# Last product of a three-stage kernel: which operand stays in the array, and how its result is stored

## The chip, the cores and the metric

One core of a Trainium2 chip runs the kernel. The metric is the device time of one execution in microseconds (us). Engines are named as the profile names them: PE (TensorE, matmul), PEld (its weight loads), DVE (VectorE), ACT (ScalarE), POOL (GpSimd), and SP (SyncE), which here only issues DMAs.

## The reference

Three stages follow each other. A chunked linear attention gives a matrix x of 3072 tokens by 256 features; two feed-forward blocks follow:

```python
h = x @ w_in                      # 3072x256 @ 256x2048
x2 = (np.maximum(h, 0)**2) @ w_out      # 2048 -> 256
a = x2 @ w1;  b = x2 @ w2         # 256 -> 1024 each
out = (a * b @ w3) @ w_out2       # 1024 -> 1024 -> 256
```

All of it is float32.

## The kernel before

**Tiles and phases.** Tokens are worked in six tiles of 512 (`TT`, `NTILE`). A tile t has a phase A of 16 steps (`h_mm` L825: 128 hidden features of the first block; `x2_mm` L856: their share of x2) and a phase B of 8 steps (`a_mm` L891, `b_mm` L899, their product, and `out_mm` L907: its share of the output). The order is A0, A1, B0, B1, then A2, B2, A3, B3 and so on to B5 (`PHASES`, L945). "Step A8" is the ninth step of a phase A. The two weights w3 and w_out2 are multiplied with each other in the kernel once (`w3_product`, L251), giving `w3o` of 1024 x 256; the last product is then (a * b) @ w3o.

**Precision.** Each operand is held as a high and a low part (`split`, L143: ACT makes the high part, DVE the rest, `split_lo`). One product is three matmuls, `PASSES` (low x high, high x high, high x low). The parts of a step's activations are a tile `gp` (L134), made by `part_hi` (ACT, L846) and `part_lo` (DVE, L141); the pool has four buffers (`GPB`), given out in turn and free again when the last reader is done.

**Order of the work.** `second` (L1162) runs the second product of a step three steps behind the first (`LAG`), so the last three `out_mm` of a tile lie in the first three steps of the next phase A (for tile 0, of B1). After the last of them `out_evac` (L937) empties the two accumulators, and the next tile's `x2_mm` takes those two PSUM banks (`ps_acc`, two buffers). The compiler's scheduler fixes each engine's order at build time from its own estimate of the times; each engine then runs its list in order, waiting on semaphores.

**The last product before.** In `out_mm` 128 tokens of `gp` are stationary and the 256 columns of `w3o` move: four groups of tokens by three passes, 12 matmuls a step. The result has tokens on the partitions, so ACT copies each accumulator to a `tmp` tile and it is stored in rows of 1 KB, two DMAs a tile. The last tile (t = 5) is finished by `out_last` (L926), group by group.

**What lies beside it.** All DMAs go to SP's queue, in program order (`dma`, L92). While the feed-forward blocks run, the attention of the next tile is made piecewise at fixed slots of the phases (`attention_plan`, L963). A unit of B and C is split into a `gp` buffer and stored to DRAM (`unit_split`, L490, tensor `hl_d`), read back in two arrangements (`unit_bc`, L533, tiles `bt` and `cb`), the decays `e` are loaded (`unit_e`, L514), masked on POOL (L556) and multiplied on DVE (L621). In phases A2, A3 and A4 the first unit of the next tile is split in step A2 (slot 4), the step of `out_evac`; the second unit's split takes a `gp` buffer at slot 13.

Of the kernel before, what the change touches and what calls it, by code (L numbers as in the profile page):

```python
# [7 lines left out]
F32 = mybir.dt.float32  # L8
# [7 lines left out]
P = 128  # L16
# [5 lines left out]
NT, DM, DFF, DF2 = NB * S, H * D, 2048, 1024  # L22
TT = 512
UT = 256
NTILE = NT // TT
KM = DM // P
# [6 lines left out]
MF2 = DF2 // P  # L33
NSUB = TT // P
# [24 lines left out]
def kernel(  # L59
# [19 lines left out]
    nc = tc.nc  # L79
# [12 lines left out]
    def dma(out, in_):  # L92
        tc.keep_in_program_order(nc.sync.dma_start(out=out, in_=in_))  # L93
# [37 lines left out]
    def new_tmp():  # L131
        return tmp.tile([P, 512], F32, tag="tmp", name="tmp")

    def new_gp():  # L134
        return gp.tile([P, 2, 512], F32R, tag="gp", name="gp")

    def new_mm():
        return ps_mm.tile([P, 512], F32, tag="mm", name="mm")

    def split_lo(hi, lo, src):  # L140
        return nc.vector.tensor_tensor(out=lo, in0=src, in1=hi.bitcast(F32), op=ALU.subtract)  # L141

    def split(hi, lo, src):  # L143
        nc.scalar.copy(hi, src)
        split_lo(hi, lo, src)
# [8 lines left out]
    wa, w12, w3, w3o = {}, {}, {}, {}  # L154
# [59 lines left out]
    def conv_parts(i):  # L214
        kind, j = PIECES[i]
        v = cv.pop(i)
        if kind == "o":
            if j == 0:
                wo2.append(act1.tile([P, N_O, 512], F32R, tag="xt", name="wo2"))
            if j % 2 == 0:  # L220
                wo2l[0] = at.tile([P, 2, 512], F32R, tag="e", name="wo2l")
            w = wo2[0][:, j], wo2l[0][:, j % 2]
            split(*w, v)
            wo2.append(w)
            return
        w = wts.tile([P, 2, 512], F32R, tag=PLACE[j % 8] if kind == "3" else f"w{kind}{j}", name=f"w{kind}{j}")
        if kind == "a" and j > 2:
            nc.gpsimd.tensor_copy(w[:, 0, :], v)
        else:
            nc.scalar.copy(w[:, 0, :], v)  # L230
        split_lo(w[:, 0, :], w[:, 1, :], v)
        KEPT[kind][j] = w
        if kind == "3" and j % 2:
            w3_product(j // 2)
# [16 lines left out]
    def w3_product(f):  # L251
        acc = new_mm()
        n = 0
        for e in range(MF2):
            v = w3[2 * f + e // 4]
            for l, r in PASSES:
                nc.tensor.matmul(  # L257
                    acc[:, :DM], v[:, l, e % 4 * P:(e % 4 + 1) * P],
                    wo2[1 + e // 2][r][:, e % 2 * DM:(e % 2 + 1) * DM],
                    start=(n == 0), stop=(n == 3 * MF2 - 1)  # L260
                )
                n += 1
        if f % 2 == 0:
            w3o[f // 2] = wts.tile([P, 2, 2, DM], F32R, tag=f"wo{f // 2}", name=f"w3o{f // 2}")
        w = w3o[f // 2]
        split(w[:, 0, f % 2, :], w[:, 1, f % 2, :], acc[:, :DM])

# [541 lines left out]
    PASSES = ((1, 0), (0, 0), (0, 1))  # L811
# [42 lines left out]
    acc = {}  # L854
# [25 lines left out]
    prods = {}  # L880
# [26 lines left out]
    def out_mm(t, m, subs=range(NSUB), done=True):  # L907
        if m == 0:
            acc["o"] = [ps_acc.tile([P, 2, DM], F32, tag="acc", name="acc") for _ in range(NSUB // 2)]
            if t == NTILE - 1:  # L910
                acc["o"] += [ps_g.tile([P, 2, DM], F32, tag="g", name="acc") for _ in range(NSUB // 2)]
        g = prods[t, m]
        per = NSUB // len(acc["o"])
        for sub in subs:
            for n, (l, r) in enumerate(PASSES):
                i = nc.tensor.matmul(  # L916
                    acc["o"][sub // per][:, sub % per, :], g[:, l, sub * P:(sub + 1) * P], w3o[m // 2][:, r, m % 2, :],
                    start=(m == 0 and n == 0 and sub % per == 0), stop=(m == MF2 - 1 and n == 2),
                    skip_group_check=True,
                )  # L920
                if not done:
                    keep(i)
        if done:
            del prods[t, m]

    def out_last(t):  # L926

        ms = [k[2] for k in late]
        late.clear()
        for sub in range(NSUB):  # L930
            for m in ms:
                out_mm(t, m, (sub,), False)
            o = new_tmp()[:, :DM]
            nc.scalar.copy(o, acc["o"][sub][:, 0])
            dma(out=out[t * TT + sub * P:t * TT + (sub + 1) * P, :], in_=o)

    def out_evac(t):  # L937
        for j in range(NSUB // 2):
            o = new_tmp().rearrange("p (s e) -> p s e", s=2)
            nc.scalar.copy(o, acc["o"][j])  # L940
            r0 = t * TT + 2 * j * P
            dma(out=out[r0:r0 + 2 * P, :].rearrange("(s p) e -> p s e", p=P), in_=o)


    PHASES = [("A", 0), ("A", 1), ("B", 0), ("B", 1)] + [(ph, t) for t in range(2, NTILE) for ph in "AB"]  # L945
# [216 lines left out]
    def second(n, flush=None):  # L1162

        while late and (len(late) > n or (flush and any(k[:2] == flush for k in late))):
            ph, t, m = late.pop(0)
            if ph == "A":
                if flush and m == MF - 2 and (ph, t) == flush:
                    late.pop(0)
                    for e in range(KM):
                        x2_mm(t, m, (e,), True)  # L1170
                        x2_mm(t, m + 1, (e,), True)
                        x2_evac(t, e)
                    continue
                x2_mm(t, m)
                if m == MF - 1:
                    for e in range(KM):
                        x2_evac(t, e)
            else:
                out_mm(t, m)
                if m == MF2 - 1:  # L1180
                    out_evac(t)
# [42 lines left out]
    for ph, t, m in SEQ:  # L1224
# [3 lines left out]
        else:  # L1228
            step(ph, t, m)
    parts()  # L1230
    out_last(NTILE - 1)


# [62 lines left out]
```

## Time and profile before

| | us |
|---|---|
| median of 3 runs | 561.94 (561.61 to 562.13) |
| the profiled execution | 561.75 |
| its span, first to last instruction | 560.0 |
| PE busy | 546.9 (98%) |
| PEld / DVE / ACT / POOL busy | 460.3 / 361.9 / 288.7 / 88.6 |
| matmuls of `out_mm` in all | 576 |
| DMA, share of 16 engines' span | 35.5% |

The profiled execution is 0.19 us below the median, and 1.75 us of it lie outside its span. A matmul's own length in the profile includes the filling and emptying of the array and overlaps the next one; the rate is read from start to start. TensorE's granted clock is 0.996 of full speed on the mean.

### The profile page before, as it was taken

To read this page: it belongs to the slowest core of one execution; us is meant where nothing else is said; L and a number is where in the kernel's file an instruction comes from. 1 tells how busy PE (TensorE), PEld (TensorE's weight loads), DVE (VectorE), ACT (ScalarE), POOL (GpSimd) and SP (SyncE) were. 2 spreads that over 40 slices of the span, in tenths; PEclk is the share of its full clock that TensorE was granted. 3 is DMA by queue.
4 is the path that set the end of the run, shared out by engine and by line. 5 is a ranking of instruction groups with operands and counts; after the bars stand their busy time and mean duration, and the time that the engine had idled before them with its cause. 6 is when DMAs were issued, how large, how long until landed. Compare 5 with 4: busy or idle time off the path is not lost.

```text
span 560.0 us, 9614 instructions
## 1 busy us (share of the span) xinstructions
PE 546.9 (98%) x3580; PEld 460.3 (82%) x3580; DVE 361.9 (65%) x655; ACT 288.7 (52%) x553; POOL 88.6 (16%) x136
## 2 busy tenths in 40 slices
PE   8979999999999999999999999999999999999997
PEld 6757777888888888888888888888888888888886
DVE  5799998977898555466476456474456574545431
ACT  6799768787884342444343444342535332544332
POOL 8264730000001240013030003020012010000000
PEclk9989999999999999999999999999999999999999
DMA  8797690253446470075250066020162220100001
GB/s 240 248 288 249 213 389 7 74 153 107 156 149 169 102 198 1 15 191 143 58 142 1 29 165 148 22 78 1 52 175 77 57 68 1 39 1 1 1 1 37
DMA packets 48735, 59.49 MB, mean 106 GB/s; under 512 B 22960, under 2 KB 36784, under 8 KB 48688
## 3 DMA queue, kind: packets, MB, share of 16 engines
q1 hardware_dynamic: 48688, 58.88, 35.5%
q8 instruction: 28, 0.46, 0.4%
q14 instruction: 19, 0.16, 0.1%
HBM read 50.20 MB, written 8.65 MB: 105 GB/s over the span
## 4 chain that ended last, share of the span: by engine, by line
PE 81%; DVE 8%; DMA 5%; ACT 3%; SPq 1%; issue 1%; DVEq 0%; ACTq 0%
PE mm L816 43%; PE acc L863 18%; PE acc L916 12%; PE mm L257 4%; PE y L752 2%; DVE gp L141 2%; PE g L615 2%; DMA hl_d<-gp 1%; DMA hl_d<-hl 1%; SPq L93 1%; DVE wa L141 1%; DMA raw<-in_raw_dram 1%; DVE cvs L207 1%; DMA u<-in_w_dram 1%; DVE cvs L210 1%
## 5 line engine op out<-in xcount | busy, mean ns | idle before, releaser
L816 PE MATMUL mm<-xt,wa 128*128 128x512 f32 x576 | 148.6, 396 | 3.2 <-DVE wa L141 2.0
L846 ACT CAST gp<-tmp 128x512 fp32r<-128x512 f32 x144 | 89.4, 621 | 115.3 <-DVE tmp L904 63.6
L863 PE MATMUL acc<-gp,wa 128*128 128x512 f32 x576 | 145.9, 392 | 1.3 <-DVE gp L141 0.7
L141 DVE TENSOR_TENSOR gp<-tmp,gp 128x512 fp32r<-128x512 f32 x144 | 103.6, 720 | 61.1 <-ACT gp L846 60.8
L816 PE MATMUL mm<-x,w 128*128 128x512 f32 x576 | 142.6, 393 | 0.0
L816 PEld LDWEIGHTS mm<-xt,wa 128*128 128x128 f32 x576 | 106.4, 190 | 25.8 <-ACT tmp L830 2.4
L863 PEld LDWEIGHTS acc<-gp,wa 128*128 128x128 f32 x576 | 106.5, 188 | 24.5 <-DVE gp L141 1.5
L816 PEld LDWEIGHTS mm<-x,w 128*128 128x128 f32 x576 | 104.5, 188 | 20.5 <-ACT tmp L896 0.2
L830 ACT ACTIVATE tmp<-mm 128x512 f32<-128x512 f32 x96 | 57.3, 596 | 50.8 <-PE mm L816 50.4
L916 PEld LDWEIGHTS acc<-w3o,gp 128*128 128x128 f32 x576 | 75.8, 190 | 4.6 <-DVE gp L141 0.3
L916 PE MATMUL acc<-w3o,gp 128*128 128x256 f32 x576 | 78.5, 283 | 0.1
L840 DVE TENSOR_TENSOR tmp<-tmp 128x512 f32<-128x512 f32 x68 | 47.5, 699 | 29.8 <-ACT tmp L830 28.5
L904 DVE TENSOR_TENSOR tmp<-tmp,mm 128x512 f32<-128x512 f32 x48 | 32.9, 686 | 48.5 <-PE mm L816 44.9
L556 POOL TENSOR_SCALAR_AFFINE_SELECT e<-e 96x768 f32<-96x768 f32 x26 | 25.8, 1005 | 235.8 <-DMA e<-e_d 228.7
L896 ACT COPY tmp<-mm 128x512 f32<-128x512 f32 x48 | 28.1, 586 | 45.9 <-PE mm L816 45.6
L575 POOL TENSOR_TENSOR xb<-xb,dec 96x256 f32<-96x256 f32 x32 | 23.1, 723 | 94.6 <-DMA xb<-in_xb_dram 93.6
L621 DVE TENSOR_TENSOR e<-g,e 128x384 f32<-128x384 f32 x52 | 27.6, 551 | 6.0 <-PE g L615 4.7
L257 PE MATMUL mm<-wo,w 128*128 128x256 f32 x128 | 23.7, 284 | 0.9 <-DVE w L141 0.9
L257 PEld LDWEIGHTS mm<-wo,w 128*128 128x128 f32 x128 | 20.6, 191 | 2.5 <-DVE w L141 1.5
L742 DVE SCALAR_TENSOR_TENSOR xb<-xb,through,y 32x64 f32<-32x64 f32 x72 | 20.4, 283 | 2.8 <-PE y L714 1.1
L615 PEld LDWEIGHTS g<-cb,bt 96*128 96x128 f32 x96 | 16.1, 190 | 2.8
L257 PE MATMUL mm<-wo2l,w 128*128 128x256 f32 x64 | 18.1, 283 | 0.0
(109 smaller groups left out, 447.2 us busy)
## 6 DMA issues: line engine op xcount, KB each, us to landing
u<-in_w_dram SPq DMA_DIRECT2D x24, 512.0 KB, 4.4
ua<-in_w_dram SPq DMA_DIRECT2D x16, 512.0 KB, 6.8
e<-e_d SPq DMA_DIRECT2D x40, 192.0 KB, 4.6
xb<-in_xb_dram SPq DMA_DIRECT2D x32, 192.0 KB, 3.7
bt<-hl_d SPq DMA_DIRECT2D x78, 48.0 KB, 2.0
hl_d<-gp SPq DMA_DIRECT2D x9, 384.0 KB, 2.5
cb<-hl_d SPq DMA_DIRECT2D x66, 48.0 KB, 2.0
out_dram<-tmp SPq DMA_DIRECT2D x10, 256.0 KB, 2.9
```

What stands on the lines that cost most here:

```text
L141: return nc.vector.tensor_tensor(out=lo, in0=src, in1=hi.bitcast(F32), op=ALU.subtract)
L257: nc.tensor.matmul(acc[:, :DM], v[:, l, e % 4 * P:(e % 4 + 1) * P], wo2[1 + e // 2][r][:, e % 2 * DM:(e % 2 + 1) * DM], start=(n == 0), st ...
L615: nc.tensor.matmul(ps[:, 2 * pp:2 * pp + 2], w, un["c2"][:, pr, :, j * CH:(j + 1) * CH], start=True, stop=True)
L621: nc.vector.tensor_tensor(out=m, in0=ps, in1=m, op=ALU.mult)
L816: i = nc.tensor.matmul(ps, w[m][:, l, col + k * P:col + (k + 1) * P], rhs[k][:, r, :], start=((l, r, k) == (1, 0, 0)), stop=((l, r, k) == ...
L830: nc.scalar.activation(r, ps, AF.Relu)
L840: nc.vector.tensor_tensor(out=g32, in0=r, in1=r, op=ALU.mult)
L846: nc.scalar.copy(g[:, 0, :], d[k])
L863: i = nc.tensor.matmul(acc["x2", t][e], wa[m][:, l, 256 + e * P:256 + (e + 1) * P], g[:, r, :], start=(m == 0 and n == 0), stop=(m == MF - ...
L896: nc.scalar.copy(s, ps)
L904: nc.vector.tensor_tensor(out=p32, in0=prods[t, m], in1=ps, op=ALU.mult)
L916: i = nc.tensor.matmul(acc["o"][sub // per][:, sub % per, :], g[:, l, sub * P:(sub + 1) * P], w3o[m // 2][:, r, m % 2, :], start=(m == 0 a ...
```

## The change

For tiles 0 to 4 `out_mm` has 128 x 128 blocks of `w3o` stationary and the 512 tokens of `gp` moving: two blocks of output features by three passes, six matmuls of 512 columns a step. The result has features on the partitions and tokens along the row. `out_evac` turns it on VectorE in 32 x 32 blocks from PSUM into one `gp` buffer and stores it by four DMAs of 32 partitions each, in runs of 256 bytes. For that the columns of `w3o` are stored in another order (in `w3_product`'s two copies), and the last tile, whose product stays as it was, puts them back in its copy.

```diff
@@ w3_product
-        split(w[:, 0, f % 2, :], w[:, 1, f % 2, :], acc[:, :DM])
+        split(
+            *(w[:, l, f % 2, :].rearrange("p (h q e) -> p h q e", h=KM, q=4) for l in range(2)),
+            acc[:, :DM].rearrange("p (q h e) -> p h q e", h=KM, q=4)
+        )
@@ out_mm
         g = prods[t, m]
+        if t < NTILE - 1:
+            for e in range(KM):
+                for n, (l, r) in enumerate(PASSES):
+                    nc.tensor.matmul(
+                        acc["o"][e].rearrange("p s e -> p (s e)"), w3o[m // 2][:, l, m % 2, e * P:(e + 1) * P],
+                        g[:, r, :], start=(m == 0 and n == 0), stop=(m == MF2 - 1 and n == 2),
+                    )
+            del prods[t, m]
+            return
@@ out_last
-            nc.scalar.copy(o, acc["o"][sub][:, 0])
+            nc.scalar.copy(
+                o.rearrange("p (q h e) -> p q h e", q=4, h=KM),
+                acc["o"][sub][:, 0].rearrange("p (h q e) -> p q h e", q=4, h=KM),
+            )
@@ out_evac
-        for j in range(NSUB // 2):
-            o = new_tmp().rearrange("p (s e) -> p s e", s=2)
-            nc.scalar.copy(o, acc["o"][j])
-            r0 = t * TT + 2 * j * P
-            dma(out=out[r0:r0 + 2 * P, :].rearrange("(s p) e -> p s e", p=P), in_=o)
+        o = new_gp().bitcast(F32).rearrange("p a b -> p (a b)").rearrange("p (b h e) -> p b h e", h=KM, e=32)
+        for e in range(KM):
+            nc.vector.transpose(o[:, :, e], acc["o"][e].rearrange("p s e -> p (s e)").rearrange("p (b i) -> p b i", i=32))
+        rows = out[t * TT:(t + 1) * TT, :].rearrange("(b i) (q e) -> q i b e", i=32, q=4)
+        for q in range(4):
+            dma(out=rows[q], in_=o[32 * q:32 * q + 32].rearrange("i b h e -> i b (h e)"))
```

## Rows read from the trace of the kernel before

**Rows 1.** Busy time by stretch: length, then PE, PEld, DVE, ACT, POOL, clock, DMA.
```profile
160.00:560.00 400.00, 396.69 (x2469) 337.67 (x2467) 224.50 (x405) 160.13 (x297) 41.60 (x60) 1.00 0.27 71
```
**Rows 2.** PE in order of time (start, length), end of B2, start of A3.
```profile
305.78 2.91 PE L816 MATMUL mm<-x,w 128*128 128x512 f32 x12
308.53 1.59 PE L916 MATMUL acc<-w3o,gp 128*128 128x256 f32 x12
309.96 1.55 PE L816 MATMUL mm<-xt,wa 128*128 128x512 f32 x6
311.35 1.59 PE L916 MATMUL acc<-w3o,gp 128*128 128x256 f32 x12
```
**Rows 3.** PE in order of time, later in A3: `h_mm` and `x2_mm` alternate.
```profile
326.61 1.52 PE L816 MATMUL mm<-xt,wa 128*128 128x512 f32 x6
...
329.33 1.52 PE L816 MATMUL mm<-xt,wa 128*128 128x512 f32 x6
```
**Rows 4.** PE in order of time, accumulators handed from tile 2 to 3.
```profile
318.42 4.27 PE L816 MATMUL mm<-xt,wa 128*128 128x512 f32 x18
...
322.53 4.24 PE L863 MATMUL acc<-gp,wa 128*128 128x512 f32 x18
```
**Rows 5.** Groups by line, whole span: count, busy us, mean ns, idle before.
```profile
L904 DVE TENSOR_TENSOR tmp<-tmp,mm 128x512 f32<-128x512 f32 x48 | 32.9, 686 | 48.5 <-PE mm L816 44.9 <-ACT xt L144 2.0 <-PE g L615 1.2
...
L206 DVE TENSOR_SCALAR u<-u 128x512 uint32<-128x512 uint32 x16 | 6.8, 425 | 6.7 <-DMA u<-in_w_dram 6.6
...
L141 DVE TENSOR_TENSOR w3o<-mm,w3o 128x256 fp32r<-128x256 f32 x8 | 3.3, 417 | 0.5 <-ACT w3o L144 0.5
...
L940 ACT COPY tmp<-acc 128x512 f32<-128x512 f32 x10 | 5.6, 590 | 0.3
```
**Rows 6.** ACT and DVE in order of time at the same hand-over.
```profile
318.76 1.07 ACT L940 COPY tmp<-acc 128x512 f32<-128x512 f32 x2
...
324.54 0.62 ACT L846 CAST gp<-tmp 128x512 fp32r<-128x512 f32 x1 [0.84 <-PE acc L863]
...
318.12 0.36 DVE L141 TENSOR_TENSOR gp<-raw,gp 128x192 fp32r<-128x192 f32 x1 [2.37 <-ACT gp L144]
...
319.60 0.35 DVE L141 TENSOR_TENSOR gp<-raw,gp 128x192 fp32r<-128x192 f32 x1
```
**Rows 7.** SP's DMA issues in order of time, same hand-over.
```profile
319.98 0.39 SPq L93 DMA_DIRECT2D hl_d<-gp  x1
320.47 1.02 SPq L93 DMA_DIRECT2D out_dram<-tmp  x2
322.56 3.69 SPq L93 DMA_DIRECT2D bt<-hl_d  x6
...
334.77 0.38 SPq L93 DMA_DIRECT2D hl_d<-gp  x1
```
**Rows 8.** ACT's and PE's step A8 in phases A2, A3 and A4.
```profile
257.94 0.62 ACT L846 CAST gp<-tmp 128x512 fp32r<-128x512 f32 x1 [4.38 <-DMA hl_d<-gp]
...
258.84 0.62 PE L863 MATMUL acc<-gp,wa 128*128 128x512 f32 x2
...
341.60 0.62 ACT L846 CAST gp<-tmp 128x512 fp32r<-128x512 f32 x1 [4.61 <-DMA hl_d<-gp]
...
342.26 0.62 PE L863 MATMUL acc<-gp,wa 128*128 128x512 f32 x2
...
420.38 0.62 ACT L846 CAST gp<-tmp 128x512 fp32r<-128x512 f32 x1 [3.19 <-DMA hl_d<-gp]
...
421.79 1.52 PE L863 MATMUL acc<-gp,wa 128*128 128x512 f32 x6
```
**Rows 9.** Stretches as in rows 1; DMA share is last but one.
```profile
322.50:331.00 8.50, 8.50 (x39) 7.03 (x38) 4.88 (x9) 4.31 (x9) 0.00 (x0) 1.00 0.46 118
331.00:341.00 10.00, 10.00 (x48) 8.36 (x47) 4.48 (x7) 2.93 (x5) 5.24 (x7) 1.00 1.01 238
...
484.00:486.00 2.00, 2.00 (x11) 1.64 (x10) 1.18 (x2) 1.20 (x3) 0.00 (x0) 1.00 0.79 262
```

## The prediction

> **What bounds the kernel now.** I read the busy times by stretch first. From 160 us on, where all tiles 0 to 4 have their last product, PE is busy 396.69 of 400 us while DVE has 224.50 and ACT 160.13 [rows 1]; the 3.3 us that PE lacks are the end of the kernel. So the sum is made on PE's time from start to start, and another engine counts only where it makes PE late. Then PE's order of time gives the rate of each kind of matmul [rows 2, 3]. Then I looked for places where PE is on time by little: the hand-over of the accumulators [rows 4, 6, 7], and, by following what ends ACT's longest waits, step A8 of phases A2 to A4 [rows 8]. The reader is to see there that ACT's cast for A8 waits over 3 us for a DMA and that PE starts on its result at once.
>
> **What PE saves.** A product of 12 matmuls of 256 columns lasts from 308.53 to 309.96, 1.43 us or 119.2 ns each; the six of 512 columns behind it last to 311.35, 1.39 us [rows 2]. Together 2.82 us. The change makes this pair one of six and six matmuls of 512 columns on 128 x 128 weights, which is what h_mm and x2_mm are in phase A: from 326.61 to 329.33, 2.72 us, 226.7 ns each [rows 3]. Saved: 0.10 us. In phase B the pair is twelve and twelve: 305.78 to 309.96, 4.18 us [rows 2], against 18 x 226.7 ns = 4.08; again 0.10. There are five tiles of eight steps: 40 x 0.10 = 4.0 us. The columns streamed are the same; what goes is 240 matmuls at 2 x 119.2 - 226.7 = 11.7 ns (2.8 us) and the slower 512-column matmuls just behind 256-column ones.
>
> The Trainium skill (TensorE: Matmul & The Clock Gate, section Back-to-back issue gap) gives a gap of N / 2.4 + 2.5 ns for isolated matmuls; by it 12 matmuls of 256 columns and six of 512 would differ by 15 ns, 0.6 us in 40 products. The rows show some 12 ns more than the columns at either width, so I go by the rows.
>
> **What the evacuation costs.** Ten ACT copies of 590 ns go [rows 5]; ACT is off the path and its gain is taken as nothing. Ten DVE transpositions of 128 x 512 out of PSUM come. No row shows one: the bounds are 425 ns (a fast DVE operation of that size) and two passes of 686 ns, 1.37 us; I take 686 ns, since that row reads PSUM [rows 5]. DVE has the room on the mean [rows 1], so only the place counts. The next tile's x2_mm may start when both are done; today the copies end at 319.83 and x2_mm starts at 322.53 [rows 4, 6], a cover of 2.7 us. I cost this wait at nothing; without the cover it would be one transposition a tile.
>
> What DVE is moved in front of is the split of the attention unit in step A2. Its second low part ends at 319.95 [rows 6], the hl_d store is issued at 319.98, and bt waits for its landing until 322.56; behind it SP issues without pause the cb, e and xb loads and the second hl_d store at 334.77 [rows 7]. From 331 us the 16 DMA engines are full (1.01) [rows 9], and the cast of A8 waits for that store's landing: 341.60, with PE starting at 342.26, 0.04 us after the cast is done [rows 8]. So a delay of the first store, or of bt, goes through to PE, less a margin. The margins: 0.04 in A3; 0.28 in A2 (257.94 + 0.62 against 258.84); about 0.5 in A4, where the cast leaves 0.79, the low part ends 0.69 later and is first wanted by the third matmul, 0.45 after the start [rows 8].
>
> How large is the delay? Its lower end is 0: before the unit's first low part DVE idles 2.37 us [rows 6], the first block's accumulator is ready half a product earlier than the second's, and transpositions put behind the split delay no store. Its upper end is two transpositions, 1.4 us, both ahead of the second low part. I take one, 0.7 us; the same comes out if both run behind the split: they end near 321.3, and four issues of about 0.5 us (1.02 for two) carry SP to 323.3, 0.7 past bt's 322.56 [rows 7]. Less the margins: 0.65 + 0.4 + 0.2 = 1.25 us in the three phases. Tiles 0 and 4 have no such split beside their evacuation; I take nothing there, and 0.7 us each if that is wrong.
>
> The result now sits in one of the four gp buffers. In A2 to A4 the parts of step A2 then get the buffer of step A0, free only after its x2 product, as A3's do today: that cast starts at 324.54 [rows 6], so the low part would end near 325.9; the product of A2 starts at 322.53 + 2 x 1.36 = 325.25 and wants it at 325.7 [rows 4]. Between 0 and 0.2 us three times; I take 0.4 in all. The buffer of the result itself is wanted by A4's parts, near 329.4; the stores, issued by 323.3 and landing as fast as hl_d (2.6 us) [rows 7], give it back near 326.
>
> The eight pairs of copies of w3_product and the last tile's copies read in runs of 32 elements: no row differs in that alone. They may cost nothing or a doubling of 0.4 us each [rows 5], of which only the last copy of the kernel lies on the path; I take 0.
>
> **Sum.** 561.75 - 4.0 + 1.25 + 0.4 = 559.4 for the profiled execution, which lies 0.19 under the median of the runs: 559.6.
>
> **The DMA packets.** A tile's output is now 2048 runs of 256 bytes instead of 512 of 1 KB. Two tile stores alone in the queues used 0.79 of 16 engines for 2 us: 25.3 us for 512 packets, 49 ns each [rows 9]. A packet of 256 bytes costs between a quarter of that (12 ns, by bytes) and all of it; I take 30 ns between them: 3.8 us of 16 engines instead of 1.6. From 322.5 to 331 the engines are 0.46 busy, 4.6 us free [rows 9], so the 2.2 us more are hidden.
>
> **Rivals.** (a) Nothing is given back: the scheduler fits the transpositions into DVE's idle time and bt stays on time. 561.94 - 4.0 = 557.9, up to 558.6. For it: the idle 2.37 us; against it: margins of 0.04 to 0.5.
> (b) Slower: the packets. From 48 ns a packet on (128 x 48 ns = 6.2 us, 4.6 more than now) the stores are not through when the e loads begin, and every further 10 ns holds up the second hl_d store, and PE at A8, by 1.3 us in three phases, 3.8 us. With the forecast's other terms the gain is gone at 54 ns and the kernel is slower by 0.2% at 57; at 64 ns it takes 565.6. For it: 49 ns for 1 KB is just past the point. Against it: four times the bytes are in that figure.
> The Trainium skill (DMA: Bandwidth & Descriptors, Specifications) asks for 512 B or more, below which a write is read-modify-write. If that doubled a packet's 49 ns, it would be (b) at its far end, 128 x 98 ns = 12.5 us and nearly 20 us lost; no row here shows stores of 256 bytes.
> (c) Everything is late: both transpositions ahead of the second low part, 1.4 us less the margins, 1.36 + 1.1 + 0.9, and A2's 0.6: 4.0 given back, 561.9, no change.
> (d) The 12 ns are not the matmul's: if the new form runs two by two like the old, only about 0.6 us are saved and 1.65 given back, 563.0. Against it: rows 3 are the same shapes.
>
> **How the numbers follow.** Forecast (558.6 to 560.8) 0.47; (a) 0.25; (b) 0.13; (c) 0.13; (d) 0.02. A change of 0.2% (1.1 us) is about what a measurement of this kernel can tell from none. Faster: (a) and nearly all of the forecast's case, 0.70. Same: (c) and the forecast's slow edge, 0.15. Slower: (b), (d): 0.15. The range for 8 in 10 goes from 557.6 to 562.6 and leaves out (b), (d) and the edges of (a).
>
> **What would show it.** PE in order of time: steps of 2.72 us in the last product's place, and 240 matmuls fewer. Transpositions near 0.69 us. The second hl_d store's issue and A8's cast, measured from the end of the tile's last product (16.35 and 23.2 us in A3 now): later by 0 for (a), 0.7 for the forecast, and PE waiting there for DVE or ACT by that less the margin. A DMA share near 1 between the stores and the e loads would show (b). The prediction is wrong if the scheduler orders other work anew and PE waits in places that have none now, or if the 512-column products take 238 ns.

## The result and the profile after

| | before | after |
|---|---|---|
| median | 562.23 us (561.61 to 565.99, 8 runs) | 557.53 us (557.23 to 559.61, 8 runs) |
| ratio | 1 | 0.9915 [0.9898, 0.9931] |
| the profiled execution, its span | 561.75, 560.0 | 559.61, 557.9 |
| PE / PEld busy | 546.9 / 460.3 | 544.0 / 448.5 |
| DVE / ACT busy | 361.9 / 288.7 | 367.6 / 284.3 |

The kernel is 4.7 us faster where 2.35 were forecast; 557.53 lies 0.07 under the range. The time is near that of rival (a), "nothing is given back" (557.9); its mechanism came only in half, as the lines below show: a transposition does fit into DVE's idle time, but `bt` isn't on time.

The profiled execution of after, 559.61, is 2.1 us above the median, and its trace shows where. PE in order of time near the kernel's start (start, length), then a stretch there as in [rows 1]:

```profile
13.29 1.00 PE L755 MATMUL mm<-e,xb 128*32 128x96 f32 x16 [1.46 <-DVE e L679]
...
15.95 1.66 PE L637 MATMUL g<-cp,bi 32*128 32x192 f32 x16
```

```profile
15.00:20.00 5.00, 5.00 (x63) 4.15 (x66) 2.93 (x8) 2.52 (x7) 2.53 (x5) 0.74 1.03 396
```

The same matmuls and stretch in experiment 8, whose PE has the same program:

```profile
12.76 0.99 PE L755 MATMUL mm<-e,xb 128*32 128x96 f32 x16 [0.86 <-DVE e L679]
...
14.65 0.93 PE L637 MATMUL g<-cp,bi 32*128 32x192 f32 x16
```

```profile
15.00:20.00 5.00, 5.00 (x92) 4.20 (x84) 2.70 (x7) 3.80 (x10) 3.07 (x7) 1.00 1.04 409
```

After an idle of 1.46 us instead of 0.86 the 16 matmuls of L637 take 1.66 us instead of 0.93, and the granted clock of the stretch is 0.74 of full speed, a mix of the levels 2.4 and 1.2 GHz; the first `out_mm` then starts at 167.91 instead of 165.72. So everything below is measured from the first `out_mm`, where the two kernels begin to differ in the loops: from it to the end of the span after takes 557.9 - 167.91 = 389.99 us, before 560.0 - 166.23 = 393.77. The change is worth 3.78 us there.

PE in order of time at the end of B2 and the start of A3, to be laid beside [rows 2, 4]:

```profile
312.38 1.52 PE L819 MATMUL mm<-xt,wa 128*128 128x512 f32 x6
313.74 1.52 PE L919 MATMUL acc<-gp,w3o 128*128 128x512 f32 x6
315.10 1.52 PE L819 MATMUL mm<-xt,wa 128*128 128x512 f32 x6
316.46 1.52 PE L919 MATMUL acc<-gp,w3o 128*128 128x512 f32 x6
317.82 4.24 PE L819 MATMUL mm<-xt,wa 128*128 128x512 f32 x18
...
321.90 2.43 PE L866 MATMUL acc<-gp,wa 128*128 128x512 f32 x10
```

The pair is 315.10 - 312.38 = 2.72 us, as forecast. From the first `out_mm` to the end of tile 1's last product it is 67.25 us after (to 235.16) against 68.77 before: 1.52 for sixteen products. From there to the end of the last product of tile 2, of 3 and of 4 it is 82.66, 81.75 and 81.62 us after (ends 317.82, 399.57, 481.19) against 83.42, 82.49 and 82.33 before: 0.71 to 0.76 for eight products. All in all that is 0.094 each. From tile 4's last one to the end of the span nothing changes: 76.71 us after, 76.76 before.

DVE, ACT and SP in order of time at this hand-over, for [rows 6, 7]:

```profile
317.34 0.72 DVE L955 STREAM_TRANSPOSE gp<-acc 128x512 f32<-128x512 f32 x1 [1.84 <-PE acc L919]
...
318.55 0.62 DVE L141 TENSOR_TENSOR gp<-raw,gp 128x192 fp32r<-128x192 f32 x2
319.08 0.72 DVE L955 STREAM_TRANSPOSE gp<-acc 128x512 f32<-128x512 f32 x1
...
317.21 0.59 ACT L144 CAST gp<-raw 128x192 fp32r<-128x192 f32 x2
...
319.20 0.39 SPq L93 DMA_DIRECT2D hl_d<-gp  x1
319.82 2.59 SPq L93 DMA_DIRECT2D out_dram<-gp  x4
322.52 3.31 SPq L93 DMA_DIRECT2D bt<-hl_d  x6
...
334.57 0.38 SPq L93 DMA_DIRECT2D hl_d<-gp  x1
```

The first transposition fills DVE's idle time, the second lies behind both low parts of the unit. ACT, without its copies, makes the two casts of the unit in one go. From the end of the product (317.82 after, 318.42 before), the first `hl_d` store is issued at 1.38 us (before 1.56), `bt` at 4.70 (4.14), the second `hl_d` store at 16.75 (16.35). So the transpositions delay no store; `bt` is 0.56 late because SP issues the four output stores ahead of it, 2.59 us where two took 1.02 [rows 7]. Then ACT and PE at the step of [rows 8]:

```profile
341.41 0.62 ACT L849 CAST gp<-tmp 128x512 fp32r<-128x512 f32 x1 [5.06 <-DMA hl_d<-gp]
...
341.64 0.62 PE L866 MATMUL acc<-gp,wa 128*128 128x512 f32 x2
...
344.64 1.52 PE L866 MATMUL acc<-gp,wa 128*128 128x512 f32 x6
```

The cast comes at 23.59 us (before 23.18), 0.41 late, and PE starts the product at 341.64 while the cast still runs: it cannot be this cast's product. PE itself has no wait from 160 to 556 us. Those of its weight loads, by what ended them (sum, count, longest):

```profile
PEld y L755 <- issue: 4.2, 12, 0.4
PEld acc L928 <- DVE gp L141: 0.3, 1, 0.3
PEld mm L819 <- ACT tmp L899: 0.2, 1, 0.2
```

In tiles 0 to 4 no product waits for a part, a store or a transposition; the 0.3 us at L928 are the last tile's, and the kernel before has them too.

### The profile page after: what moved, and what is told of

Same layout as the page of the kernel before. It is cut to its first block, busy times and chain, and to the rows that moved or that the text cites. A ratio compares the mean times of both kernels' runs of the same rounds, so it can differ in the third digit from the quotient of the medians.

```text
span 557.9 us, 9140 instructions
## 1 busy us (share of the span) xinstructions
PE 544.0 (98%) x3340; PEld 448.5 (80%) x3340; DVE 367.6 (66%) x665; ACT 284.3 (51%) x543; POOL 88.1 (16%) x136
## 4 chain that ended last, share of the span: by engine, by line
PE 81%; DVE 8%; ACT 4%; DMA 4%; issue 1%; SPq 1%; DVEq 0%; ACTq 0%
PE mm L819 43%; PE acc L866 19%; PE acc L919 10%; PE mm L257 4%; PE acc L928 2%; PE y L755 2%; PE g L618 2%; DVE gp L141 2%; DMA xb<-in_xb_dram 1%; DMA raw<-in_raw_dram 1%; DVE cvs L207 1%; DVE wa L141 1%; SPq L93 1%; DVE cvs L210 1%; DMA u<-in_w_dram 1%
## 5 line engine op out<-in xcount | busy, mean ns | idle before, releaser
L819 PEld LDWEIGHTS mm<-x,w 128*128 128x128 f32 x576 | 105.9, 188 | 21.7 <-ACT tmp L899 0.2
L919 PE MATMUL acc<-gp,w3o 128*128 128x512 f32 x240 | 63.7, 391 | 0.0
L919 PEld LDWEIGHTS acc<-gp,w3o 128*128 128x128 f32 x240 | 44.8, 188 | 9.4
L618 PEld LDWEIGHTS g<-cb,bt 96*128 96x128 f32 x96 | 16.6, 190 | 3.3
```

The source lines that it names most:

```text
L618: nc.tensor.matmul(ps[:, 2 * pp:2 * pp + 2], w, un["c2"][:, pr, :, j * CH:(j + 1) * CH], start=True, stop=True)
L819: i = nc.tensor.matmul(ps, w[m][:, l, col + k * P:col + (k + 1) * P], rhs[k][:, r, :], start=((l, r, k) == (1, 0, 0)), stop=((l, r, k) == ...
L919: nc.tensor.matmul(acc["o"][e].rearrange("p s e -> p (s e)"), w3o[m // 2][:, l, m % 2, e * P:(e + 1) * P], g[:, r, :], start=(m == 0 and n ...
```

## The experiments

Each ratio is to executions of the kernel before that were taken along with the run.

**1. The changed kernel once more**, with no edit.

> The changed kernel unaltered, for a second profile. Its profiled execution was 2 us above the median of its runs, and its first out_mm began 1.7 us later than that of the kernel before, so a part of the 4.7 us between the medians is unaccounted for. If the PE rate is the whole gain (40 pairs of 0.10 us), a profile at the median shows the stretch from the first out_mm to the end 3.8 to 4.0 us shorter than before and the remaining 0.7 to 0.9 us before the first out_mm. If something is gained behind it as well, that stretch is 4.5 us shorter or more.

558.23 us (557.55 to 561.06), ratio 0.9942 [0.9924, 0.9960]. So the gain is between 3.7 and 4.7 us by the medians of two sets; its profiled execution (559.67) begins 2 us late like the first.

**2. The product alone.** The new product, with the evacuation of before:

```diff
     def out_evac(t):
-        o = new_gp().bitcast(F32)...
...
+        for j in range(NSUB // 2):
+            o = new_tmp().rearrange("p (s e) -> p s e", s=2)
+            nc.scalar.copy(o, acc["o"][j])
```

> The new product with the evacuation of before: two ACT copies and two stores of 1 KB rows a tile, the result not turned (its output rows hold features by tokens). Theory A, the gain is PE's alone and the evacuation costs nothing: same time as the changed kernel within 0.5 us, some 4 to 4.7 us under the kernel before. Theory B, the evacuation gives back what was forecast (1.25 + 0.4 us) and the product gains more than 4.0: 1 to 2 us under the changed kernel.

557.83 us (557.24 to 558.79), 0.9926 [0.9914, 0.9938]: the whole gain, not to be told from that of the whole change. From its first `out_mm` (165.53) to the end of its span (555.6) it takes 390.07 us, against 389.99 for the whole change: transpositions and stores of 256 bytes take nothing of the gain.

**3. The evacuation alone.** The old product, with the transpositions and the stores of the change:

```diff
-        if t < NTILE - 1:
-            for e in range(KM):
...
-            del prods[t, m]
-            return
         per = NSUB // len(acc["o"])
```

> The product of before (12 matmuls of 256 columns) with the new evacuation, 32x32 blocks turned on VectorE and four stores in runs of 256 bytes (the output is permuted, since the product was not swapped). Theory A: within 0.5 us of the kernel before. Theory B: 1.25 to 1.65 us slower than the kernel before.

562.38 us (561.58 to 562.68), 1.0004 [0.9995, 1.0012]. The three stretches from product end to product end are 83.42, 82.48 and 82.34 us, those of before. The one from the first `out_mm` to tile 1's last is 69.54 (166.27 to 235.81) against 68.77, and the weight loads have one wait more. It and SP's issues around it:

```profile
202.86 0.16 PEld L717 LDWEIGHTS y<-xb,pb 96*32 96x32 f32 x8 [0.76 <-POOL pb L578]
...
194.83 4.18 SPq L93 DMA_DIRECT2D cb<-hl_d  x6
199.12 0.84 SPq L93 DMA_DIRECT2D xb<-in_xb_dram  x2
...
205.80 2.18 SPq L93 DMA_DIRECT2D out_dram<-gp  x4
```

POOL's step waits for an `xb` load that is issued at 199.12, 0.94 us later than before (198.18), because six `cb` issues ahead of it take 4.18 us instead of 3.28. Tile 0's four stores are issued only at 205.80, when the wait is over. So this is not the 0.7 that the prediction put against tile 0 "if wrong"; why the `cb` issues take longer was not found. In the changed kernel the wait is not there.

**4. Twice as many matmuls.** The changed kernel, each matmul of 512 columns as two of 256 on the same weights:

```diff
-                    nc.tensor.matmul(
-                        acc["o"][e].rearrange("p s e -> p (s e)"), ..., g[:, r, :], ...
+                    for c in range(2):
+                        nc.tensor.matmul(
+                            acc["o"][e][:, c], ..., g[:, r, c * 256:(c + 1) * 256], ...
```

> The changed kernel with each matmul of 512 columns cut into two of 256 on the same weights; same columns, same operands, same evacuation. If the gain is a fixed cost of some 12 ns a matmul, the 40 pairs of 0.10 us are lost again: 4.0 us slower than the changed kernel, and 12 matmuls take 1.43 us from start to start. If the gain is from the swap of the operands, it stays within 0.5 us of the changed kernel. By the fixed 2.5 ns of the Trainium skill (TensorE: Matmul & The Clock Gate, Back-to-back issue gap) it would lose 0.6 us; that figure is an estimate from the page.

561.9 us (561.41 to 565.23), 1.0002 [0.9990, 1.0015]. PE in order of time:

```profile
166.15 1.60 PE L920 MATMUL acc<-gp,w3o 128*128 128x256 f32 x12
167.59 2.91 PE L819 MATMUL mm<-x,w 128*128 128x512 f32 x12
```

Twelve take 1.44 us, 120 ns each, what they took before with the operands the other way round (119.2); in phase A the six of 512 columns behind them take 1.38 us again (310.13 to 311.51), and the pair 2.82. The gain is gone, though operands, columns and evacuation are those of the change: within the interval it comes from the 240 matmuls fewer and nothing else, by the fixed part of each (2.8 us) and by the 512-column matmuls that no longer stand behind 256-column ones (the rest). By the gap for isolated matmuls in the Trainium skill (TensorE: Matmul & The Clock Gate, section Back-to-back issue gap) the estimate was 0.6 us; the runs have nearly 4.

**5 and 6. A transfer pushed in.** To delay the second `hl_d` store in A2 to A4, one or three transfers of 512 KB ahead of it:

```diff
+    def push(t):
+        for k in range(1):        # 3 in the other run
+            sink = dram.tile([P, 4 * DM], F32, name=f"sink{t}{k}")
+            dma(out=sink, in_=w3o[k].bitcast(F32).rearrange("p a b e -> p (a b e)"))
...
+        if p0[0] == "A":
+            put0(13, push, t)
```

> The changed kernel with one further transfer of 512 KB (one tile of w3o to a DRAM tensor that nobody reads) in the queue just ahead of the second hl_d store in phases A2, A3 and A4; the queue is full there, so the store lands some 2.2 us later (512 KB at 232 GB/s). The prediction read the cast that waits for that store as step A8's, with margins of 0.04 to 0.5 us; so read, PE loses 2.2 less 0.2, three times, about 6 us. Counted cast by cast and product by product the cast belongs to A9 (A8 in phase A4), whose product starts 3.2 us after the cast does and whose low part is in time by 2.3 us: so read, nothing is lost, within 0.5 us of the changed kernel, with the cast's wait 2.2 us longer.

557.57 us (557.00 to 559.75), 0.9906 [0.9883, 0.9929]: nothing lost.

> The same with three such transfers, 1.5 MB, some 6.6 us of a full queue. By the reading of the prediction (no margin) three times 6.4, about 19 us slower than the changed kernel. By the count of casts and products the store uses up 2.3 us of margin first: three times 4.3, about 13 us slower, and PE waits in phases A2, A3 and A4 in front of the product of A9 (A8 in A4). If nothing is lost here either, the store does not reach PE at all.

559.75 us (558.36 to 561.44), 0.9955 [0.9938, 0.9972]: some 2 us lost where 13 or 19 were expected. Neither run tested what it was meant to. With one transfer the scheduler gave the buffer to another step: A9's cast ran at 338.31 without waiting, and the one that waited for `hl_d` (343.76) was A10's, 3.3 us before its product. ACT in order of time:

```profile
338.31 0.62 ACT L849 CAST gp<-tmp 128x512 fp32r<-128x512 f32 x1 [1.61 <-DVE tmp L843]
343.76 0.62 ACT L849 CAST gp<-tmp 128x512 fp32r<-128x512 f32 x1 [3.96 <-DMA hl_d<-gp]
```

With three, neither A9's nor A10's cast waits for `hl_d`; the one that does is A14's, at 353.02. The loss is at the attention's `cb`, wanted by L618 before it was loaded: the waits of PE and of its weight loads have

```profile
PE g L618 <- DMA cb<-hl_d: 1.4, 1, 1.4
...
PEld g L618 <- issue: 2.0, 2, 1.8
```

So the four buffers don't simply go round in turn: a transfer that the scheduler can see, and puts into its own times, changes who gets which and who waits. The delay had to be one that it can't see, and that is what runs 8 and 9 are.

**7. The last tile too.** The sixth tile's product in the new form, its end evacuated by two transpositions:

```diff
-        for sub in range(NSUB):
+        for e in range(KM):
             for m in ms:
-                out_mm(t, m, (sub,), False)
-            o = new_tmp()[:, :DM]
...
+                out_mm(t, m, (e,), False)
+        out_evac(t)
```

> The changed kernel with the sixth tile's last product swapped as well, finished one block of features after the other and then turned and stored like the rest. PE saves eight more products of 0.09 us, 0.75 us. The end of the kernel grows: today one ACT copy of 0.37 us and one store stand behind the last matmul, here one transposition of 0.71 us and four stores, issued at 0.5 us each and landing later: 1.5 to 2.5 us more. Net 1 to 2 us slower than the changed kernel. If the stores' tail is shorter than read, it is up to 0.75 us faster.

561.29 us (560.79 to 561.82), 0.9978 [0.9967, 0.9989]: 3.1 to 3.8 us worse than the change, where 1 to 2 were expected. The end of its trace, all engines in order of time:

```profile
550.81 0.72 DVE L937 STREAM_TRANSPOSE gp<-acc 128x512 f32<-128x512 f32 x1 [0.59 <-PE acc L916]
552.88 0.72 DVE L937 STREAM_TRANSPOSE gp<-acc 128x512 f32<-128x512 f32 x1 [1.35 <-PE acc L916]
553.62 2.20 SPq L93 DMA_DIRECT2D out_dram<-gp  x4
```

Four issues of half a microsecond and transfers of 256-byte runs now stand behind the last matmul: the span ends at 559.1, 5.5 us behind the last transposition. After ends 2.8 us behind its last copy (554.77 + 0.37 to 557.9), with three of its four stores already issued. What is free in the middle is paid in full at the end.

**8 and 9. Shorter runs.** The changed kernel, its output written in runs of 128 and of 64 bytes. ACT's order in A2 to A4, with its waits, is that of the changed kernel in both; PE's and DVE's are the same in run 8 and differ by single instructions in run 9 (the edit shown is run 8's; run 9 has `e=16` for `e=32`):

```diff
-        rows = out[t * TT:(t + 1) * TT, :].rearrange("(b i) (q e) -> q i b e", i=32, q=4)
+        flat = out[t * TT:(t + 1) * TT, :].rearrange("a b -> (a b)").rearrange("(c i q e) -> q i c e", i=32, q=4, e=32)
         for q in range(4):
-            dma(out=rows[q], in_=o[32 * q:32 * q + 32].rearrange("i b h e -> i b (h e)"))
+            dma(out=flat[q], in_=o[32 * q:32 * q + 32].rearrange("i b h e -> i (b h e)").rearrange("i (c e) -> i c e", e=32))
```

> The changed kernel with each tile's output written in 4096 runs of 128 bytes instead of 2048 of 256 (the numbers land in another order of places; nothing else differs, and ACT, PE and DVE keep the order of the changed kernel exactly). It delays the transfers without moving any other instruction, as the pushed transfers of the earlier runs did not. If a packet of 128 bytes costs what one of 256 does (18.7 ns), a tile's stores take 4.8 us of the 16 engines, 2.4 more. Margin by counting (the cast that waits for hl_d is A9's, with 2.3 to 2.6 us to its product): the share between the stores and the e loads rises from 0.52, nothing reaches PE, 557.5 to 558.2. The prediction's margin (step A8, 0.04 to 0.5 us): whatever delay the second hl_d store or its landing gets, up to 2.4 us, is lost in three phases, 559 to 564.

558.10 us (557.45 to 558.34), 0.9928 [0.9916, 0.9940]. ACT at the waiting cast:

```profile
340.46 0.62 ACT L849 CAST gp<-tmp 128x512 fp32r<-128x512 f32 x1 [6.29 <-DMA hl_d<-gp]
```

The product ended at 315.63, so the cast is at 24.83, 1.24 us later than in the changed kernel, and PE loses nothing: the stretch that holds A3, from tile 2's last product to tile 3's, is 81.76 us (81.75), and 389.98 pass from the first `out_mm` to the end (389.99). By the prediction's margin of 0.04 it would have lost 1.2 us in A3 alone.

> The same with 8192 runs of 64 bytes a tile (ACT's order in phases A2 to A4 is unchanged, PE's differs by single matmuls that change places). At 12 to 18.7 ns a packet the stores take 6.1 to 9.6 us of 16 engines, 3.7 to 7.2 more than at 256 bytes; the engines have 4.1 us free between the stores and the full stretch, so the landing that the cast waits for comes 0 to 3.1 us late. Margin by counting, 2.3 to 2.6 us: 557.5 to at most 560, and where PE waits, it waits in step A9 of A2 to A4 and only by what the landing is late beyond 2.3 us. The prediction's margin: three times the whole delay, up to 567. This is also the prediction's rival of the packets, pushed past the point from which it was to decide.

561.19 us (559.39 to 564.78), 0.9991 [0.9976, 1.0006]. Here the cast is at 343.50 - 317.31 = 26.19, 2.60 later, and now its product waits. ACT, PE and its weight loads:

```profile
343.50 0.62 ACT L849 CAST gp<-tmp 128x512 fp32r<-128x512 f32 x1 [7.65 <-DMA hl_d<-gp]
...
341.79 1.12 PE L866 MATMUL acc<-gp,wa 128*128 128x512 f32 x4
...
344.17 1.93 PE L866 MATMUL acc<-gp,wa 128*128 128x512 f32 x6
...
344.17 0.30 PEld L866 LDWEIGHTS acc<-gp,wa 128*128 128x128 f32 x2 [0.31 <-ACT gp L849]
344.90 0.77 PEld L866 LDWEIGHTS acc<-gp,wa 128*128 128x128 f32 x4 [0.43 <-DVE gp L141]
```

A8's product is over before the cast is (its last four matmuls start at 341.79). A9's, at 344.17, starts 0.05 us behind the cast's end, where the changed kernel has 2.61; its weight loads wait 0.31 us for the high part and 0.43 for the low one, and it lasts 1.93 us instead of 1.52. So the margin in A3 is 2.60 less 0.4, some 2.2 us, where 0.04 was read. From the first `out_mm` to the end the run loses 558.6 - 166.21 - 389.99 = 2.4 us: 0.9 up to tile 1's last product, 0.3, 0.5 and 0.7 in the three stretches. The 0.3 and the 0.5 lie mainly at A9's product (1.82 us in A2 and 1.93 in A3, for 1.52); A8's in A4 loses 0.1, and the rest of the 0.7, like the 0.9, is at the attention's L618, whose weight loads wait 0.9 us in B1 and 0.7 in A4. Its median is 3.0 to 3.7 above the changed kernel's two; the rest lies ahead of the first `out_mm` or between executions and stays open.

Both runs also price a packet. Run 8's stretches hold nothing but tile 4's stores (length, busy times, clock, DMA share, GB/s):

```profile
481.00:482.00 1.00, 1.00 (x6) 0.81 (x6) 1.00 (x3) 0.24 (x2) 0.00 (x0) 1.00 0.57 89
482.00:483.00 1.00, 1.00 (x6) 0.84 (x5) 0.60 (x2) 0.58 (x1) 0.00 (x0) 1.00 0.94 143
483.00:484.00 1.00, 1.00 (x7) 0.81 (x6) 0.39 (x2) 0.60 (x1) 0.00 (x0) 1.00 0.97 143
484.00:485.00 1.00, 1.00 (x6) 0.84 (x5) 0.61 (x1) 0.00 (x0) 0.00 (x0) 1.00 0.94 142
485.00:486.00 1.00, 1.00 (x6) 0.84 (x5) 0.00 (x0) 0.41 (x1) 0.00 (x0) 1.00 0.06 8
```

3.48 x 16 = 55.7 us for 4096 packets, 13.6 ns each; run 9 gives 3.11 x 2 x 16 = 99.5 us for 8192, 12.1 ns. That last figure is a mean of two rates: the share is about 0.9 at first and 1.6 to 1.9 in the last 1.5 us, more than one packet at a time on an engine. The changed kernel itself:

```profile
483.00:484.00 1.00, 1.00 (x6) 0.83 (x5) 1.00 (x3) 0.41 (x1) 0.00 (x0) 1.00 0.31 71
484.00:485.00 1.00, 1.00 (x6) 0.84 (x5) 0.61 (x2) 0.60 (x1) 0.00 (x0) 1.00 0.68 152
485.00:486.00 1.00, 1.00 (x6) 0.81 (x6) 0.49 (x1) 0.53 (x1) 0.00 (x0) 1.00 0.96 198
486.00:487.00 1.00, 1.00 (x6) 0.84 (x5) 0.69 (x1) 0.07 (x1) 0.00 (x0) 1.00 0.44 104
```

2.39 x 16 = 38.2 us for 2048 packets of 256 bytes, 18.7 ns, against 49 ns for 1 KB [rows 9].

## Why the prediction was wrong

**What PE saves: right in kind, 0.2 us high.** 4.0 were forecast from 40 products at 0.10; from the first `out_mm` to the end it is 3.78, 0.094 each. Run 4 shows that the saving is in the number of matmuls, as the prediction had it, and the pair's 2.72 us rule out rival (d). Which 0.2 us are missing was not found.

**The give-back at "step A8": the step that failed.** 1.25 us were charged because the cast of 341.60 ends 0.04 us before the product of 342.26 starts [rows 8]. The two were paired because they are near in time. They don't belong together. The casts of A3 in order, ACT of the kernel before:

```profile
329.58 0.62 ACT L846 CAST gp<-tmp 128x512 fp32r<-128x512 f32 x1 [0.81 <-PE acc L863]
332.30 0.62 ACT L846 CAST gp<-tmp 128x512 fp32r<-128x512 f32 x1 [0.81 <-PE acc L863]
335.02 0.62 ACT L846 CAST gp<-tmp 128x512 fp32r<-128x512 f32 x1 [0.81 <-PE acc L863]
```

and its products, PE of the kernel before:

```profile
336.33 1.54 PE L863 MATMUL acc<-gp,wa 128*128 128x512 f32 x6
339.30 1.52 PE L863 MATMUL acc<-gp,wa 128*128 128x512 f32 x6
...
345.27 1.52 PE L863 MATMUL acc<-gp,wa 128*128 128x512 f32 x6
```

Counted from the start of the phase, the casts at 329.58, 332.30 and 335.02 are A6, A7 and A8, and the products at 336.33, 339.30 and 342.26 are A6, A7 and A8 too: the product of 342.26 uses the cast of 335.02. The waiting cast is A9's, for the product of 345.27, 3.05 us behind its end. The names of the tiles in the built program say the same:

```
ACT  L846 CAST gp_4007<-tmp_3977 128x512
PE   L863 MATMUL acc_3798<-gp_4007,wa9_900 128x512
```

`wa9` is step 9's weights, so [rows 8] pair A9's cast with A8's product. In A2 it is A9 as well (257.94 for 261.85); in A4 it is A8 (420.38 for 424.51), paired there with A7's product; the true distances are 3.3 and 3.5 us. The delay itself was sized about right, and by the second of the two ways that the prediction gave, the four issues on SP: 0.7 forecast, 0.56 at `bt`, 0.41 at the cast. With a margin of 2 to 3 us in place of 0.04 to 0.5, all of it is hidden. Runs 8 and 9 show that directly for A3: 1.24 us of delay cost nothing, 2.60 us cost 0.4 at the product. Runs 5 and 6 left it open. Rival (a) had the right time for another reason, no delay at all; that its number came is luck in part.

**A2's cast and the four buffers: 0.4 forecast, nothing measured.** PE shows no such wait. The count was off by one here too: the cast of 324.54 [rows 6], read as A3's, is A4's. In the changed kernel A2's cast waits for the `hl_d` store (321.86) and A3's for A0's product (323.91), and the scheduler runs the first `x2_mm` in another order, ten matmuls at 321.90 where 18 stood in a row at 322.53 [rows 4]; A2's product starts at 326.43, when its low part is long done (323.21).

**Tiles 0 and 4 at nothing: right.** PE has no wait beside either evacuation. Run 3's wait of 0.8 us lies near tile 0's, but ahead of its stores, and is not the alternative that was priced.

**Transposition: 686 ns forecast, 710 measured**, and the cover of 2.7 us held it: the second ends at 319.80, `x2_mm` starts at 321.90.

**Packets: 30 ns forecast, 18.7 measured.** Rival (b) decided from 48 ns on. Hidden either way; run 9 had to cut the runs to a quarter to bring a loss. The Trainium skill (DMA: Bandwidth & Descriptors, section Specifications) has transfers below 512 bytes done as read-modify-write. The estimate of 98 ns for that case is far from the 18.7 measured; no run here shows whether such a write is done in two steps.

**Copies in runs of 32 elements: nothing, as forecast.** The last tile's copies are 0.37 us in both kernels, the parts of `w3o` 421 ns on DVE against 417 [rows 5].

**The range.** Without the 1.65 us the sum would have been 561.94 - 4.0 = 557.9, within the range. The rest to 557.53 is probably ahead of the first `out_mm`, which starts between 165.53 and 166.52 in the profiled executions of these kernels that don't begin 2 us late, 0.5 us earlier in run 8 than before. That is argued, not shown: no profile of the changed kernel without the late start was taken. No cause was found for the spread, and the range had no term for it.

## What to carry to other kernels

A margin is between an operation and its own consumer: count both lists from a common start, or follow the tile's name, before a nearness in time is taken for dependence. A matmul of 4-byte data has a fixed part next to its columns (12 ns here), so the operand with the longer free side should move; turning the result round cost next to nothing in mid-kernel and 3 to 4 us behind the last matmul. To measure a margin, add a delay that the scheduler can't see, since one that it sees moves the waits.

## What was not expected of the hardware

- Packets to DRAM took 49, 18.7 and 13.6 ns of an engine at 1024, 256 and 128 bytes. These lie on a line of about 8.5 ns a packet and 0.04 ns a byte, so bytes, not packets, made up most of the time down to 256 bytes. At 64 bytes the mean was 12.1 ns, with packets overlapping late in the transfer.
- A matmul of 256 columns costs 119 to 120 ns whichever operand is stationary ([rows 2], experiment 4), one of 512 costs 226.7 ns, before [rows 3] and after.
- PE idle for 1.46 us instead of 0.86 near the kernel's start went with a granted clock of 0.74 from 15 to 20 us and with all later work 2 us late. It is not the program's doing alone: of the eight executions in the first set this one took 559.61 us at a mean clock of 0.993, the others 557.23 to 557.88 at 0.996 to 1.000; in run 1 two of six had 0.993.
